# Three edits to a written order: a pair's tail rows stored by GpSimd instead of ScalarE, another pair's stored earlier on the SP queue, and one narrowing step ahead of a copy

## The chip, the core and the metric

The kernel runs on one core of a Trainium2 chip. The core's engines (TensorE for matrix products, VectorE, ScalarE, GpSimd, and SyncE, whose queue issues most of the DMAs) each take their own instructions in order and wait for one another through semaphores. The metric is the device time of one execution in microseconds (us). Where several executions are timed, the median is given. A profile is one execution with a record of every instruction; its times start at the first instruction of the span. In its rows PE is TensorE's matrix product, PEld its weight load, DVE VectorE, ACT ScalarE, POOL GpSimd, SP SyncE, and a q behind the name (SPq, ACTq) is the engine's sequencer, which issues DMAs.

## The reference

Attention without a softmax, with a normalisation per head, followed by a gated linear unit with a causal convolution of five taps. There are 8 sequences (batch) of 576 tokens, 8 heads of 64, so 512 channels.

```
kv  = einsum('bhsd,bhse->bhde', k, v)
out = einsum('bhsd,bhde->bhse', q, kv)
x   = out / sqrt(mean(out*out, -1) + 1e-6) * g_norm     # heads side by side: (8, 576, 512)
gate_pre = sum over k of conv_w[k] * x shifted by 4 - k tokens
y   = (sigmoid(gate_pre) * (x @ w_val)) @ w_out
```

q, k, v and g_norm are float32; the three weights come as float64, which the kernel narrows itself.

## The kernel before

The whole kernel is a list of steps, PLAN (lines 19 to 226), written out by hand in one order. A loop at line 882 calls one small function for each step, so the list's order is the order in which each engine gets its instructions, and nothing is rescheduled. A step such as `store 0 8` is the function with its arguments; numbers behind an @ pick the buffers that the step's new tiles take.

Work goes by sequence b (0 to 7) and, from the output product on, by pairs i (0 to 3) of two sequences. For one sequence: load_half and load_q bring k, v and q; kv_product and kv_copy make kv; turn_q transposes q on VectorE; raw_pair and raw_tail make out in chunks c of 128 tokens (chunk 4 is the tail of 64); square (ScalarE), sums (VectorE) and powers (GpSimd) give the norms and normalise scales; turn_blocks (VectorE) and move_blocks b a (line 663: four DMAs, two issued by GpSimd and two by SP) put the transposed x of tokens 128 a to 128 a + 127 into xT, while the tail goes through TensorE (turn_x, keep_x, then halo). Then gate_start, gate_tap and gate_end make the gate. x_sums, val_fast and val_keep make x @ w_val with seven products of half size where a plain split takes eight; val_fast 3 1 0, the first of sequence 3, reads tokens 0 to 287 of xT. gated multiplies the two.

For a pair of sequences the output product works likewise: token_sums, fast_product i p n (line 818, seven products n for each of four p) and fast_keep i p n (line 841), which copies or adds a bank into one of the ot buffers. Of these there are four, numbered 0 to 3, of 128 x 512. The tails of both sequences of a pair, 64 tokens each, go together as c = 8: out_product i 8 (L784), keep_out i 8 (L792), which copies them into an ot buffer, and a store.

A store is four DMAs of 32 rows (64 KB each). It is issued by SP unless a queue is given. The step that next writes the same ot buffer must wait until all four have landed:

- first pair: keep_out 0 8 takes ot buffer 0, and fast_keep 0 2 1 (L851, ScalarE) takes it next. In PLAN store 0 8 stands on line 106, behind load_half k 5 1 and move_blocks 3 2, which issue on SP too.
- last pair: keep_out 3 8 takes ot buffer 1, and fast_keep 3 3 1 (L851) takes it next. store_side 3 8 on line 222 issues its four DMAs on ScalarE's queue, ahead of fast_keep 3 3 0 (L849) on the same engine. That copy takes ot buffer 2, which store 3 1 reads before, and the products behind it need the bank that it copies out. store_last (line 862) splits the last two stores between SP and ScalarE.

The weights are narrowed at the start by steps narrow_weight key tile n: n = 0 and n = 4 to 7 on VectorE, n = 1 to 3 on ScalarE. keep_cw (line 452) is three small VectorE operations that copy the transposed convolution weights and the column gcol out of a bank; gcol is read by n = 7 of wval (L425).

Of the kernel before, what the change touches and what calls it, by code (L numbers as in the profile page):

```python
# [27 lines left out]
narrow_weight cw 0 5 @ 0; narrow_weight cw 0 6 @ 1; raw_half 0 2 0 @ 4; narrow_weight cw 0 7;  # L28
narrow_weight wval 0 1; raw_half 0 3 1; narrow_weight wval 0 5 @ 2; raw_half 0 0 1; narrow_weight wval 0 6 @ 3;
square 0 3 @ 0; raw_half 0 4 1 @ 6; square 0 0 @ 1; turn_cw @ 1; sums 0 3 @ 0 0; raw_half 0 2 1;  # L30
narrow_weight wval 0 2; keep_cw; raw_half 0 4 0; powers 0 3; narrow_weight wval 1 0 @ 0; load_half v 1 0;
square 0 2 @ 2; raw_half 0 1 0 @ 5; sums 0 0; square 0 4 @ 0; narrow_weight wval 0 3;
narrow_weight wval 1 5 @ 0; raw_half 0 1 1; sums 0 4; start_warm 1 256 @ 0; narrow_weight wval 1 1;
load_half k 1 0; sums 0 2; square 0 1 @ 1; narrow_weight wval 0 4; powers 0 2; narrow_weight wval 1 2;
# [65 lines left out]
gate_start 2 3 @ 2; turn_blocks 3 1; token_sums 0 1 0 @ 0; square 3 4 @ 2; out_product 0 8 @ 3;  # L100
load_half k 5 0 @ 0; gate_start 2 1 @ 1; turn_q 4 1; kv_copy 4 0; kv_copy 4 1; sums 3 4; token_sums 0 1 1;
turn_q 4 3; val_keep 2 1 5; turn_blocks 3 3; raw_pair 4 1 @ 7 6; keep_out 0 8 @ 0; token_sums 0 1 3 @ 2;
move_blocks 3 1; val_keep 2 0 5; raw_pair 4 3 @ 4 2; gate_tap 2 1 3; square 4 0 @ 0; store 0 2; powers 3 4;
fast_product 0 2 0 @ 3; sums 4 0 @ 0 0; square 4 2 @ 1; gate_tap 2 3 3; gate_start 2 0 @ 3; powers 4 0;
fast_product 0 3 0 @ 0; load_half k 5 1 @ 0; gate_tap 2 1 2; fast_keep 0 2 0 @ 2; move_blocks 3 2;
normalise 3 4 @ 1; fast_product 0 2 2; token_sums 0 1 2; square 4 1 @ 2; gate_tap 2 2 3; store 0 8;
fast_product 0 3 1 @ 1; fast_keep 0 3 0 @ 1; fast_keep 0 2 2; gate_tap 2 0 3; square 4 3 @ 0;
fast_product 0 3 2; normalise 4 0 @ 0; sums 4 1; move_blocks 3 0; fast_product 0 3 3; gate_tap 2 2 2;
powers 4 1; fast_product 0 2 1 @ 5; sums 4 2; fast_keep 0 3 2; fast_keep 0 3 1 @ 3; gate_tap 2 0 2;
# [120 lines left out]
def kernel(  # L230
# [11 lines left out]
    nc = tc.nc  # L242
# [62 lines left out]
    wval = const.tile([P, NK, C], FP32, name="wval")  # L305
# [559 lines left out]
    def store(i, c, queue=nc.sync, blocks=range(HB)):  # L865
        ot = st["ot", i, c]
        for j in blocks:
            bb, n = divmod(c * HB + j, NJ * HB) if c < 2 * NJ else (j // 2, NJ * HB + j % 2)
            queue.dma_start(out=rows_out[2 * i + bb, n], in_=ot[j * TB:(j + 1) * TB, :])  # L869

    def store_side(i, c):
        store(i, c, nc.scalar)

    steps = {f.__name__: f for f in (
        load_half, load_q, load_q_rows, stage_weight, narrow_weight, turn_cw, keep_cw, start_warm, warm_up,
# [1 line left out]
        turn_x, keep_x, turn_blocks, move_blocks, halo, gate_start, gate_tap, gate_end, val_product, keep_val, gated,  # L877
        val_sums, x_sums, val_fast, val_keep, out_product, keep_out, weight_sums, token_sums, fast_product, fast_keep,
        store, store_side, store_last)}
    with tc.manual_schedule():  # L880
        set_up()
# [35 lines left out]
```

## Time and profile before

| what | us |
|---|---|
| median of three runs | 301.51 (301.21 to 302.94) |
| the profiled execution | 302.35 |
| its span, first to last instruction | 300.6 |
| DMA: share of 16 engines' time, hardware queue of SP | 56.7% |
| DMA: the same, GpSimd's software queue | 4.6% |
| DMA: the same, ScalarE's hardware queue | 2.2% |

The profiled execution is 0.84 us longer than the median of the runs, and 1.75 us of it lie around the span. A share of busy time is a mean over stages with different limits, so what an edit is worth is read at its place. The chain of waits follows the work that ended last back from the end: each piece is what released the one behind it, so time outside the chain is not time that the end waits for.

### The profile page before, as it was taken

What the parts mean: (1) busy time and instruction counts of PE and PEld (TensorE: products, weight loads), DVE (VectorE), ACT (ScalarE), POOL (GpSimd) and SP (SyncE); (2) the same over time, 40 slices, a digit from 0 to 9 for tenths busy, and PEclk for the clock granted to TensorE, in tenths of its full rate; (3) what the DMA queues carried; (4) which work ended last, traced back from release to release, by engine and by line L of the source; (5) the groups of instructions that cost most, each with busy time, mean ns of one, the idle gap of its engine ahead of it and who ended that gap; (6) DMA issues with size and microseconds to landing.
All of it is one profiled execution on the core that took longest, in us unless ns stands there. A gap on an engine that the chain in (4) does not pass through costs nothing.

```text
span 300.6 us, 8644 instructions
## 1 busy us (share of the span) xinstructions
PE 288.7 (96%) x3279; PEld 225.6 (75%) x3279; DVE 270.4 (90%) x483; ACT 198.5 (66%) x621; POOL 116.9 (39%) x127
## 2 busy tenths in 40 slices
PE   7988999999999998999999999999999999999993
PEld 4766788878887766788887767788877588788572
DVE  1699999999999998989999999998999999999712
ACT  2899999999685865883587476656567654614230
POOL 3056064862666059310692486040593081000000
PEclk9999999999999999999999999999999999999999
DMA  7999984886599558985969479653651162230344
GB/s 269 379 388 410 257 253 141 247 266 203 131 249 289 155 137 225 240 229 123 276 166 306 97 197 328 167 142 106 142 129 37 26 152 68 55 88 0 87 118 111
DMA packets 32073, 55.51 MB, mean 185 GB/s; under 512 B 6166, under 2 KB 14358, under 8 KB 32032
## 3 DMA queue, kind: packets, MB, share of 16 engines
q1 hardware_dynamic: 29328, 49.50, 56.7%
q0 software_dynamic: 1632, 3.17, 4.6%
q10 hardware_dynamic: 1072, 2.29, 2.2%
q8 instruction: 26, 0.43, 0.7%
q14 instruction: 15, 0.12, 0.1%
HBM read 39.21 MB, written 9.44 MB: 162 GB/s over the span
## 4 chain that ended last, share of the span: by engine, by line
PE 57%; DVE 16%; DMA 8%; ACT 6%; SPq 6%; issue 3%; POOL 2%; ACTq 1%; DVEq 0%
PE bank L746 22%; PE bank L837 18%; PE bank L697 6%; DVE gate L685 5%; DMA qs<-in_q_dram 5%; PE bank L475 4%; SPq L869 4%; DMA out_dram<-ot 3%; PE bank L550 3%; PE bank L784 2%; SPq L357 2%; POOL rt L616 2%; DVE ss L606 2%; ACT qT L533 1%; ACT x L635 1%
## 5 line engine op out<-in xcount | busy, mean ns | idle before, releaser
L685 DVE SCALAR_TENSOR_TENSOR gate<-xT,cwT,gate 128x576 f32<-128x576 f32 x128 | 100.1, 808 | 0.3
L616 POOL TENSOR_TENSOR rt<-ss,mhalf 128x8 f32<-128x8 f32 (+3 forms) x38 | 70.7, 1878 | 56.3 <-DVE ss L606 56.1
L635 ACT ACTIVATE x<-bank,rt 128x64 f32<-128x64 f32 x252 | 57.0, 414 | 2.3 <-POOL rt L616 2.3
L668 POOL DMA_DIRECT2D xT<-y x48 | 26.7, 561 | 73.0 <-issue 28.4
L837 PE MATMUL bank<-wsum,w 128*128 128x256 f32 x192 | 46.8, 381 | 0.6 <-ACT ot L849 0.6
L837 PEld LDWEIGHTS bank<-wsum,w 128*128 128x128 f32 x192 | 36.0, 190 | 7.2 <-ACT ot L849 1.1
L746 PE MATMUL bank<-xs,vsum 128*128 128x288 f32 x144 | 38.0, 409 | 0.1
L746 PEld LDWEIGHTS bank<-xs,vsum 128*128 128x128 f32 x144 | 26.9, 190 | 8.1 <-ACT gv L755 0.5
L697 PE MATMUL bank<-xT,wval 128*128 128x288 f32 x128 | 32.8, 409 | 0.0
L837 PE MATMUL bank<-wout,gv 128*128 128x256 f32 x128 | 32.7, 383 | 0.0
L692 ACT ACTIVATE gate<-gate 128x576 f32<-128x576 f32 x32 | 22.7, 719 | 12.8 <-DVE gate L685 12.8
L599 ACT ACTIVATE sq<-bank 128x256 f32<-128x256 f32 (+1 forms) x70 | 22.4, 401 | 9.5 <-PE bank L550 9.4
L697 PEld LDWEIGHTS bank<-xT,wval 128*128 128x128 f32 x128 | 23.7, 190 | 6.3 <-DVE wval L425 0.2
L847 DVE TENSOR_TENSOR ot<-bank,ot 128x256 f32<-128x256 f32 (+1 forms) x32 | 17.2, 548 | 12.3 <-PE bank L837 6.2
L679 ACT ACTIVATE gate<-xT,cwT 128x576 f32<-128x576 f32 x32 | 25.6, 823 | 2.4 <-DMA xT<-y 1.1
L837 PEld LDWEIGHTS bank<-wout,gv 128*128 128x128 f32 x128 | 23.8, 190 | 3.6
L606 DVE TENSOR_REDUCE ss<-sq 128x8 f32<-128x520 f32 (+1 forms) x40 | 24.9, 630 | 1.4 <-ACT sq L599 1.0
L746 PE MATMUL bank<-xT,wval 128*128 128x288 f32 x96 | 25.7, 408 | 0.1
L710 DVE TENSOR_TENSOR gv<-gv,gate 128x576 f32<-128x576 f32 x32 | 23.3, 750 | 0.6 <-ACT gate L692 0.6
L746 PEld LDWEIGHTS bank<-xT,wval 128*128 128x128 f32 x96 | 17.9, 190 | 4.9 <-issue 0.5
L550 PEld LDWEIGHTS bank<-kv,qT 64*64 64x64 f32 x1008 | 16.5, 135 | 5.4 <-issue 2.8
L475 PEld LDWEIGHTS bank<-v,k 64*64 64x64 f32 x1008 | 16.1, 135 | 3.7 <-issue 2.5
(90 smaller groups left out, 460.8 us busy)
## 6 DMA issues: line engine op xcount, KB each, us to landing
qs<-in_q_dram SPq DMA_DIRECT2D x96, 140.0 KB, 4.1
out_dram<-ot SPq DMA_DIRECT2D x136, 64.0 KB, 1.8
k<-in_k_dram SPq DMA_DIRECT2D x14, 576.0 KB, 5.8
v<-in_v_dram SPq DMA_DIRECT2D x12, 576.0 KB, 5.7
xT<-y SPq DMA_DIRECT2D x48, 64.0 KB, 2.5
xT<-y POOLq DMA_DIRECT2D x48, 64.0 KB, 2.7
y<-in_moe_w_val_dram SPq DMA_DIRECT2D x4, 512.0 KB, 11.9
w<-in_moe_w_out_dram SPq DMA_DIRECT2D x4, 512.0 KB, 10.2
```

The lines of the kernel that those rows point to most:

```text
L475: nc.tensor.matmul(st["kvps", b][s][r * D:(r + 1) * D, i], st["k", b, i][rows, r, cols], st["v", b, i][rows, r, cols], start=(j == 0), sto ...
L550: nc.tensor.matmul(st["raw", b, c][r][cols, to * D:(to + 1) * D], st["qT", b][rows, hp, first:first + D], kvs[b % 2][rows, hp, :], start=T ...
L606: nc.vector.reduce_sum(out=st["ss", b][:, FIRST[c]:FIRST[c] + n], in_=st["sq", b, c][:, 0:n], axis=AX.X)
L616: nc.gpsimd.tensor_tensor(out=st["rt", b][:, which], in0=st["ss", b][:, which], in1=mhalf[:, which], op=ALU.pow)
L635: nc.scalar.activation(out=x[:, to * D:(to + 1) * D], in_=raw[:, h * D:(h + 1) * D], func=AF.Copy, scale=root[:, to:to + 1])
L668: (nc.sync if i % 2 else nc.gpsimd).dma_start(out=xTs[b % 2][i * TB:(i + 1) * TB, :, first:first + P], in_=y[a * TB:(a + 1) * TB, i])
L679: nc.scalar.activation(out=gate[:], in_=xTs[b % 2][:, jt, HALO:SX], func=AF.Copy, scale=cwT[:, K - 1, jt:jt + 1])
L685: nc.vector.scalar_tensor_tensor(out=gate[:], in0=xTs[b % 2][:, jt, tap * TB:tap * TB + S], scalar=cwT[:, tap, jt:jt + 1], in1=gate[:], op ...
L697: nc.tensor.matmul(val[:], wval[:, kc, jt * P:(jt + 1) * P], xTs[b % 2][:, kc, HALO + n * SV:HALO + (n + 1) * SV], start=(kc == 0), stop=( ...
L710: nc.vector.tensor_tensor(out=both, in0=both, in1=st["gate", b, jt][:], op=ALU.mult)
L746: nc.tensor.matmul(st[bank, "val", b, mj][:], weights_[:, k], tokens()[:, k], start=(n in (0, 1, 3) and k == 0), stop=(k == NK // 2 - 1), ...
L837: nc.tensor.matmul(st[bank, i, p], tokens()[:, k], weights_[:, k], start=(n < 2 and k == 0), stop=(k == NK // 2 - 1), skip_group_check=True)
```

## The change

Two steps of the list move and one function changes; the same operations are done, in the same buffers.

- store 0 8 moves up, from behind gate_tap 2 2 3 to directly behind store 0 2. On SP it passes load_half k 5 1 and the two SP moves of move_blocks 3 2.
- keep_cw moves down, past raw_half 0 4 0, powers 0 3 and narrow_weight wval 1 0. On VectorE it passes one instruction, the n = 0 step of that weight (L399).
- store_side, used once for the last pair's tails, issues on GpSimd's queue instead of ScalarE's.

```
-narrow_weight wval 0 2; keep_cw; raw_half 0 4 0; powers 0 3; narrow_weight wval 1 0 @ 0; load_half v 1 0;
+narrow_weight wval 0 2; raw_half 0 4 0; powers 0 3; narrow_weight wval 1 0 @ 0; keep_cw; load_half v 1 0;
...
-move_blocks 3 1; val_keep 2 0 5; raw_pair 4 3 @ 4 2; gate_tap 2 1 3; square 4 0 @ 0; store 0 2; powers 3 4;
-fast_product 0 2 0 @ 3; sums 4 0 @ 0 0; square 4 2 @ 1; gate_tap 2 3 3; gate_start 2 0 @ 3; powers 4 0;
-fast_product 0 3 0 @ 0; load_half k 5 1 @ 0; gate_tap 2 1 2; fast_keep 0 2 0 @ 2; move_blocks 3 2;
-normalise 3 4 @ 1; fast_product 0 2 2; token_sums 0 1 2; square 4 1 @ 2; gate_tap 2 2 3; store 0 8;
+move_blocks 3 1; val_keep 2 0 5; raw_pair 4 3 @ 4 2; gate_tap 2 1 3; square 4 0 @ 0; store 0 2; store 0 8;
+powers 3 4; fast_product 0 2 0 @ 3; sums 4 0 @ 0 0; square 4 2 @ 1; gate_tap 2 3 3; gate_start 2 0 @ 3;
+powers 4 0; fast_product 0 3 0 @ 0; load_half k 5 1 @ 0; gate_tap 2 1 2; fast_keep 0 2 0 @ 2; move_blocks 3 2;
+normalise 3 4 @ 1; fast_product 0 2 2; token_sums 0 1 2; square 4 1 @ 2; gate_tap 2 2 3;
...
     def store_side(i, c):
-        store(i, c, nc.scalar)
+        store(i, c, nc.gpsimd)
```

TensorE's order is unchanged. VectorE's changes by the one instruction, ScalarE's list is shorter by the four DMAs and GpSimd's longer by them, behind its last other work; SP's changes only around the moved store.

## The prediction

> **What bounds the kernel now.** I read the busy shares first, then stretches of the span, then the chain of waits in the two places where the diff moves a store, then the queues around them.
>
> ```profile
> span 300.6 us, 8644 instructions
> PE 288.7 (96%) x3279; PEld 225.6 (75%) x3279; DVE 270.4 (90%) x483; ACT 198.5 (66%) x621; POOL 116.9 (39%) x127
> ...
> 110.00:130.00 20.00, 18.66 (x167) 15.26 (x164) 18.11 (x29) 14.19 (x57) 12.96 (x16) 1.00 0.86 220
> 130.00:190.00 60.00, 59.94 (x664) 46.31 (x663) 59.13 (x103) 38.19 (x128) 29.82 (x33) 1.00 0.76 211
> ...
> 270.00:300.60 30.60, 25.41 (x114) 18.99 (x112) 15.72 (x27) 8.06 (x20) 0.00 (x0) 0.99 0.30 78
> ```
>
> The first two lines are of the page, the other three a view by stretch (length, then busy time of PE, PEld, DVE, ACT, POOL, the granted clock, the DMA share, GB/s). TensorE is busy 96% of the span and in the middle (130 to 190 us) all but 0.06 us of 60, with VectorE all but 0.87. So there is little to gain except where TensorE stands still: 1.34 us between 110 and 130 us, and the last stretch. Both are places of this change.
>
> **The first pair's tails (store 0 8).** These rows are the chain, then timelines of TensorE, VectorE and SP.
>
> ```profile
> 116.33 3.35 DMA out_dram<-ot
> ...
> 119.82 0.38 ACT ot L851
> ...
> 115.29 2.75 PE L837 MATMUL bank<-wsum,w 128*128 128x256 f32 x12
> ...
> 120.25 1.13 PE L837 MATMUL bank<-wout,w 128*128 128x256 f32 x4 [1.34 <-ACT ot L851]
> ...
> 122.43 2.18 PE L746 MATMUL bank<-xT,wval 128*128 128x288 f32 x8
> ...
> 127.24 1.28 PE L475 MATMUL bank<-v,k 64*64 64x64 f32 x72
> ...
> 120.22 0.42 DVE L847 TENSOR_TENSOR ot<-bank,ot 128x256 f32<-128x256 f32 x1 [0.85 <-ACT ot L851]
> ...
> 129.31 0.42 DVE L606 TENSOR_REDUCE ss<-sq 128x4 f32<-128x260 f32 x1 [1.03 <-ACT sq L599]
> ...
> 112.86 0.52 SPq L347 DMA_DIRECT2D k<-in_k_dram  x1
> 113.43 1.24 SPq L668 DMA_DIRECT2D xT<-y  x2
> 114.77 2.15 SPq L869 DMA_DIRECT2D out_dram<-ot  x4
> 116.96 2.92 SPq L668 DMA_DIRECT2D xT<-y  x4
> ```
>
> The copy at L851 (fast_keep 0 2 1) writes the ot buffer that keep_out 0 8 filled, so it waits until store 0 8 has landed, at 116.33 + 3.35 = 119.68. TensorE's next product waits for that copy: 1.34 us idle, VectorE 0.85. The product that the copy reads is the first third of the group at 115.29, 2.75 / 3 = 0.92 us long, so the copy could start near 116.2.
>
> ```profile
> L869 SPq DMA_DIRECT2D out_dram<-ot x4: 425/500/591, 114.8 to 116.3; - x4
> ...
> DMA to landing us min/median/max: 3.3/3.8/4.3
> ...
> L869 SPq DMA_DIRECT2D out_dram<-ot x4: 420/545/1612, 109.5 to 112.3; - x4
> ...
> DMA to landing us min/median/max: 1.9/2.7/3.6
> ...
> k<-in_k_dram SPq DMA_DIRECT2D x14, 576.0 KB, 5.8
> ...
> xT<-y SPq DMA_DIRECT2D x48, 64.0 KB, 2.5
> ```
>
> The edit puts the four issues in the slot at 112.86. At 0.50 us each (their median) the last starts at 112.86 + 3 x 0.50 = 114.36. Landing then takes between the 1.9 us of the store just ahead and the 4.3 us that these very DMAs took behind the load of k; I take 2.7, the median of the store just ahead, since the two would be neighbours: landed at 117.1. At 4.3 it is 118.7. TensorE is due 1.34 us before 120.25, at 118.9, and the copy lies 0.43 us ahead of it (119.82 to 120.25), so it must start by 118.5. At 2.7 the whole 1.34 us go; at 4.3 the copy starts at 118.8 (0.14 us after landing, as now) and TensorE at 119.2, so 1.0 us go.
>
> What is moved past: the load of k (one issue, 0.52) and SP's two moves of move_blocks 3 2 now issue up to 2.15 us later, the length of the four issues in their old place. SP runs from 112.86 to 119.88 without a gap, so its four moves at 116.96 keep their place. The load starts at about 115 and lands 5.8 later, at 120.8; kv_product 5 1 wants it at 127.24 - 1.34 = 125.9, so 5 us cover that. The moves issue from about 115.6 to 116.2 and land 2.5 later, by 118.7; the first product that reads them is that at 122.43, which then comes at 121.1, so 2.4 us cover them. Of the later four, the first two (move_blocks 3 0) feed the same product: the second issues at about 116.96 + 2.92 / 4 = 117.7 and lands at 120.2, a cover of only 0.9 us; the other two carry tokens 384 to 511, which that product doesn't read. GpSimd's half of move_blocks 3 2 is on its own queue and isn't moved past.
>
> Who is late next? VectorE gains 0.85 here, and at 129.31 it waits 1.03 us for a square that TensorE's product releases. With both 1.34 earlier, it arrives 0.85 earlier and waits 0.54, so the whole 1.34 us is kept there. After that neither has slack to lose against the other, and SP itself waits for VectorE:
>
> ```profile
> SPq L668 <- DVE y L660: 5.8, 2, 4.7
> ```
>
> A 4.7 us wait of the DMA queue between 118 and 175 us means that the queue isn't what sets the pace there, and moves along. I take **1.3 us**, between 1.0 and 1.34.
>
> **The last pair's tails (store_side 3 8).** The chain near the end, the landing of the last DMA ahead of it, TensorE, ScalarE, and GpSimd's DMAs of the whole run:
>
> ```profile
> 287.62 0.37 ACTq L869
> ...
> 290.98 0.38 ACT ot L849
> ...
> 291.41 4.60 PE bank L837 x20
> ...
> L869 SPq DMA_DIRECT2D out_dram<-ot x1: 435/435/435, 287.1 to 287.1; - x1
> ...
> DMA to landing us min/median/max: 3.5/3.5/3.5
> ...
> 291.41 1.13 PE L837 MATMUL bank<-wsum,w 128*128 128x256 f32 x4 [0.58 <-ACT ot L849]
> ...
> 294.10 1.03 PE L837 MATMUL bank<-wout,w 128*128 128x256 f32 x4
> ...
> 293.44 0.37 ACT L851 COPY ot<-bank 128x256 f32<-128x256 f32 x1 [0.49 <-PE bank L837]
> ...
> L668 POOL DMA_DIRECT2D xT<-y x48: 551/551/638, 77.5 to 246.9; - x48
> ...
> DMA to landing us min/median/max: 2.0/2.7/5.5
> ```
>
> ScalarE spends 287.62 to about 290.9 issuing the four stores, and the copy L849 (fast_keep 3 3 0) stands behind them. That looks like 3.3 us, but is not. First, TensorE has other work: it idles only 0.58 us before 291.41, the ceiling. Second, the same copy writes the ot buffer of store 3 1, whose last DMA was issued at 287.1 and took 3.5 us to land, 290.6. So with ScalarE free it starts near 290.7 instead of 290.98: **0.3 us**, the floor, unless that landing too comes down towards the usual 1.8 us of a store, in which case 0.58. Part of its 3.5 us may be the four ScalarE stores beside it; part is not known from these rows. I take 0.35, and from there it reaches the end: the chain goes on with 20 products in one piece, and the last stores follow them.
>
> The added side: four GpSimd issues at 0.55 us from 287.7, the last at 289.35, landing 2.7 later at 292.1. GpSimd has no work at all after 270 us (the third stretch above), so nothing queues behind them but the kernel's end, and the end is over 7 us away. Who waits is fast_keep 3 3 1 (L851 at 293.44, then 293.1), which writes the same ot buffer: 1 us of cover.
>
> Here a rule speaks against the edit. The Trainium skill, "SBUF — State Buffer", section "SBUF: two separate sides", says that GpSimd cannot write the descriptors of its DMAs while VectorE runs an operation in a two-port mode, such as a float32 copy from SBUF to SBUF, and advises the ScalarE or SP queue.
>
> ```profile
> 287.46 0.42 DVE L847 TENSOR_TENSOR ot<-bank,ot 128x256 f32<-128x256 f32 x1 [3.68 <-DMA out_dram<-ot]
> 290.00 0.69 DVE L847 TENSOR_TENSOR ot<-bank,ot 128x512 f32<-128x512 f32 x1 [2.11 <-PE bank L837]
> ```
>
> If by that rule both of these held GpSimd for their whole length, the last landing would come 1.11 us later, 293.2, and cost 0.1 of the 0.35; they are additions with one operand from a bank, and no row here shows the rule at work.
>
> **keep_cw and the narrowing step.** On VectorE the three small operations of keep_cw, from 17.05 on, and the narrowing step behind them change places:
>
> ```profile
> 17.05 0.16 DVE L454 TENSOR_SCALAR gcol<-bank 128x1 f32<-128x1 f32 x1
> ...
> 17.59 0.43 DVE L399 TENSOR_SCALAR wexp<-y 128x512 uint32<-128x512 uint32 x1
> ...
> 21.61 0.73 DVE L425 SCALAR_TENSOR_TENSOR wval<-ot,gcol,wexp 128x512 f32<-128x512 f32 x1
> ```
>
> The block keeps its length, gcol is late by 0.43 us and is first read at 21.61, nearly 4 us on. The narrowing step comes 0.54 earlier (17.59 to 17.05), but stage after stage of its weight waits for ScalarE in an order that isn't changed. Zero; for a bound I take one such small operation, 0.16, either way.
>
> **Sum.** 1.3 + 0.35 + 0 = 1.65 us. The profiled execution took 302.35 us, its span 300.6 and 1.75 around it; less 1.65 is 300.7. The median of the runs is 301.51, 0.84 below the profiled one; less 1.65 it is **299.9**.
>
> **Rivals.**
>
> 1. The gain near 119 us is given back, by moves of x that land late or by a load of q or v that TensorE and VectorE now reach 1.3 us sooner. For: the DMA share there is 0.86, and the landing times above reach 4.3. Against: the covers of 0.9 to 5 us, and SP's own waits. Only the end's 0.35 is left: 301.2.
>
> 2. Slower than before: GpSimd's stores land late and hold up fast_keep 3 3 1. The place is L851 at 293.44, the product at 294.10 behind it. The first GpSimd DMAs of the run, after idleness like this, have this row:
>
> ```profile
> cw<-in_g_norm_dram POOLq DMA_DIRECT2D x2, 0.2 KB, 5.9
> ```
>
> At 5.9 the last lands at 295.25, L851 starts at 295.4, its product at 295.4 + 0.43 = 295.8, which is 1.7 after 294.10; with 1.3 gained before, 0.4 slower: 301.9. It ends slower than before once the landing passes 5.5 us, and with the first gain lost as well it is 303.2. Against: the median is 2.7, and DMA is 0.30 busy at the end.
>
> 3. The edit at the end removes nothing, since the landing of store 3 1 stays the last to come and GpSimd's packets delay it as ScalarE's did: 301.51 - 1.3 = 300.2, inside the forecast.
>
> **How the numbers follow.** The forecast, with rival 3 in it, gets 0.68 (299.5 to 300.4 with the terms' bounds and a few tenths of scatter), rival 1 0.17, rival 2 0.09, and 0.06 goes to what no row shows, half each way. The range 299.1 to 302.0 takes the forecast, rival 1 and most of rival 2. A measurement of this kernel can tell a difference of about 1%, 3 us: no gain worked out here is so large (1.34 + 0.58 = 1.92 at most), and only rival 2 with the first gain lost comes near it on the other side. So within 1% 0.90, faster 0.04, slower 0.06.
>
> **What would show it.** In the changed profile: SP's four stores directly behind those of store 0 2, landing by 118.5; no wait of TensorE for L851 near 119; VectorE's wait before L606 near 128 about 0.5; the stretch from there to 270 shifted by 1.3 as a whole; L849 no longer behind stores, but still behind the landing of store 3 1, TensorE's wait before it 0.2 to 0.3; GpSimd's four issues near 286.4 to 288.6, landing ahead of L851. It is wrong if a new wait of TensorE or VectorE over 0.3 us appears between 119 and 180, or if L851 names a DMA near the end.

## The result and the profile after

| | before | after |
|---|---|---|
| median of 21 runs each, us | 301.61 (299.82 to 304.72) | 300.22 (298.35 to 303.43) |
| ratio after / before, 95% interval | | 0.9952 (0.9932 to 0.9972) |
| the profiled execution, us | 302.35 | 299.51 |
| its span, us | 300.6 | 297.7 |

The change gains about 0.5%, 1.45 us (0.0048 x 301.61). That is inside the 1% called no change in the prediction, but the interval doesn't reach 1.

The page of after begins so:

```profile
span 297.7 us, 8649 instructions
PE 287.1 (96%) x3279; PEld 225.1 (76%) x3279; DVE 270.5 (91%) x483; ACT 198.6 (67%) x621; POOL 120.3 (40%) x131
```

The view by stretch of after (length, busy time of PE, PEld, DVE, ACT, POOL, granted clock, DMA share, GB/s):

```profile
110.00:130.00 20.00, 19.03 (x171) 15.82 (x167) 18.59 (x30) 14.93 (x59) 15.47 (x16) 1.00 0.88 231
130.00:190.00 60.00, 59.94 (x672) 46.27 (x674) 59.52 (x104) 38.49 (x129) 28.80 (x33) 1.00 0.73 206
270.00:297.70 27.70, 23.37 (x105) 17.31 (x103) 14.26 (x24) 6.84 (x16) 2.02 (x4) 1.00 0.33 86
```

TensorE still idles 0.97 us between 110 and 130 us (20 - 19.03), where 1.34 were to go whole. TensorE's timeline of after shows that this is another wait:

```profile
119.62 1.03 PE L837 MATMUL bank<-wout,gv 128*128 128x256 f32 x4
...
121.83 2.18 PE L746 MATMUL bank<-xT,wval 128*128 128x288 f32 x8 [0.97 <-DMA xT<-y]
```

The first group, the product behind the copy L851, waited 1.34 us before; it has no wait in brackets now. The group of val_fast 3 1 0 behind it waits 0.97 us for a move of x. VectorE's timeline says the same:

```profile
119.32 0.42 DVE L847 TENSOR_TENSOR ot<-bank,ot 128x256 f32<-128x256 f32 x1
...
128.71 0.42 DVE L606 TENSOR_REDUCE ss<-sq 128x4 f32<-128x260 f32 x1 [1.41 <-ACT sq L599]
```

Its 0.85 us at L847 are gone, and its wait for the square is 1.41 where it was 1.03. Time taken out at one wait has gone into the next; TensorE's 0.97 us is a new wait of over 0.3 us between 119 and 180 us, which the prediction named as a sign of being wrong. SP's timeline, and the moves' issues with their landing:

```profile
109.53 5.30 SPq L869 DMA_DIRECT2D out_dram<-ot  x8
114.93 0.40 SPq L347 DMA_DIRECT2D k<-in_k_dram  x1
115.37 3.86 SPq L668 DMA_DIRECT2D xT<-y  x6
119.28 0.60 SPq L347 DMA_DIRECT2D v<-in_v_dram  x1
```

```profile
L668 SPq DMA_DIRECT2D xT<-y x6: 585/598/607, 115.4 to 118.6; - x6
...
DMA to landing us min/median/max: 3.2/4.2/4.8
```

(The three numbers are minimum, median and maximum, of the issue in ns and of the landing in us.) The eight stores stand together, the load of k next, and all six moves directly behind it. They land 4.2 us after issue, not 2.5.

At the end the profiled execution shows most of what could be had. Rows of TensorE, of ScalarE, of the last DMA of store 3 1 and of GpSimd's stores, each from its own view of after:

```profile
288.99 1.13 PE L837 MATMUL bank<-wsum,w 128*128 128x256 f32 x4 [0.21 <-ACT ot L849]
```

```profile
288.57 0.37 ACT L849 COPY ot<-bank 128x256 f32<-128x256 f32 x1 [3.02 <-DMA out_dram<-ot]
```

```profile
L869 SPq DMA_DIRECT2D out_dram<-ot x1: 432/432/432, 285.0 to 285.0; - x1
...
DMA to landing us min/median/max: 3.4/3.4/3.4
```

```profile
L869 POOL DMA_DIRECT2D out_dram<-ot x4: 498/504/532, 285.8 to 287.4; - x4
...
DMA to landing us min/median/max: 1.9/2.3/2.8
```

The copy L849 no longer stands behind issues; it stands behind the landing of store 3 1, which again takes 3.4 us (285.04 + 3.43 = 288.47 in the chain). TensorE waits 0.21 for it, 0.58 before. GpSimd's stores have all landed by 287.4 + 2.8 = 290.2 at the latest, ahead of the copy L851.

Where the 2.9 us of span between the two profiles went is read from the start of the same TensorE product in both. Up to 118 us they agree; the first product of val_fast 3 1 0 comes 0.60 sooner (122.43 before, 121.83 after), a product at 220 us 2.08 sooner, that behind L849 2.42 sooner (291.41, 288.99), the end 2.9. So half of it, 1.5 us, arises between 122 and 220 us, where the diff changes nothing; TensorE's idle time in 130 to 222 us (92 less busy) is 0.91 before and 0.06 after. The experiments say how far that is the change's.

### The profile page after: what moved, and what is told of

Same layout as the page of the kernel before. It is cut to its first block, busy times and chain, and to the rows that moved or that the text cites. A ratio compares the mean times of both kernels' runs of the same rounds, so it can differ in the third digit from the quotient of the medians.

```text
span 297.7 us, 8649 instructions
## 1 busy us (share of the span) xinstructions
PE 287.1 (96%) x3279; PEld 225.1 (76%) x3279; DVE 270.5 (91%) x483; ACT 198.6 (67%) x621; POOL 120.3 (40%) x131
## 3 DMA queue, kind: packets, MB, share of 16 engines
q0 software_dynamic: 1760, 3.43, 5.1%
## 4 chain that ended last, share of the span: by engine, by line
PE 79%; DMA 7%; DVE 5%; SPq 3%; POOL 2%; ACT 2%; issue 1%; ACTq 0%; DVEq 0%
PE bank L837 28%; PE bank L746 28%; PE bank L697 6%; PE bank L475 5%; PE bank L784 5%; PE bank L550 4%; DMA v<-in_v_dram 4%; POOL rt L616 2%; DMA out_dram<-ot 1%; PE bank L562 1%; DMA xT<-y 1%; PE bank L647 1%; DMA qs<-in_q_dram 1%; DVE ss L606 1%; SPq L668 1%; DVE gate L685 1%
## 5 line engine op out<-in xcount | busy, mean ns | idle before, releaser
L847 DVE TENSOR_TENSOR ot<-bank,ot 128x256 f32<-128x256 f32 (+1 forms) x32 | 17.2, 548 | 10.5 <-PE bank L837 9.5
L550 PE MATMUL bank<-kv,qT 64*64 64x64 f32 x1008 | 18.4, 221 | 0.3 <-ACT x L635 0.2
```

What stands on the lines that cost most here:

```text
L550: nc.tensor.matmul(st["raw", b, c][r][cols, to * D:(to + 1) * D], st["qT", b][rows, hp, first:first + D], kvs[b % 2][rows, hp, :], start=T ...
```

## The experiments

The theory: the store's new place removes the wait at L851, but the load of k now starts just ahead of the moves of x that TensorE needs next, and they land behind it. Rivals: the moves are late whatever the place of k; or the wait removed was not the store's but only the execution's. At the end: GpSimd takes ScalarE's issues out of the copy's way, and the landing of store 3 1 is what remains; the rival is that the edit there does nothing.

Idle times are TensorE's: in 110 to 130 us (20 less busy), in 130 to 222 us (92 less busy), and the wait before the product behind L849. They are of one profiled execution each. Medians and ratios are of the timed runs, and a ratio is taken against runs of the kernel before on the same chip. The kernels were not all timed on one chip, so kernels are compared by their ratios and not by their medians.

| kernel | median us (runs) | ratio, 95% interval | 110-130 | 130-222 | behind L849 |
|---|---|---|---|---|---|
| before | 301.61 (21) | | 1.34 | 0.91 | 0.58 |
| before, once more | 302.64 (1) | | 1.89 | 0.72 | 0.65 |
| before + keep_cw moved | 302.09 (12) | 1.0006 (0.9983 to 1.0029) | 1.63 | 0.63 | 0.48 |
| before + GpSimd's stores | 301.12 (12) | 0.9988 (0.997 to 1.0006) | 1.05 | 0.85 | 0.43 |
| before + store 0 8 moved | 300.32 (12) | 0.9963 (0.9939 to 0.9987) | 0.04 | 0.89 | 0.35 |
| after | 300.22 (21) | 0.9952 (0.9932 to 0.9972) | 0.97 | 0.06 | 0.21 |
| after, once more | 299.77 (1) | | 0.81 | 0.55 | none |
| after, k behind the moves | 299.75 (12) | 0.9942 (0.9913 to 0.9972) | 2.09 | 0.47 | 0.41 |
| after, k early | 299.11 (9) | 0.9933 (0.991 to 0.9955) | 0 | 0.31 | 0.20 |
| before, k early | 299.41 (5) | 0.9923 (0.9895 to 0.9951) | 0 | 0.36 | 0.43 |
| after, store 3 1 earlier | 299.04 (1) | | 0.37 | 0.45 | none |
| after, last tails on SP | 301.00 (10) | 0.998 (0.9958 to 1.0002) | 0.46 | 0.02 | 0.22 |
| after, k early, store 3 1 earlier | 298.41 (6) | 0.9892 (0.9863 to 0.9921) | 0 | 0.01 | none |
| the same, last tails on ScalarE | 299.28 (10) | 0.9929 (0.9904 to 0.9954) | 0 | 1.21 | 0.39 |

Six ratios lie outside the range that was expected of them: keep_cw moved by 0.0001, k behind the moves by 0.0002, the last one by 0.0004, last tails on SP (slower than expected), and before with k early and after with both further moves (faster). Each measured interval still reaches into the expected range.

### Each edit by itself

Only store 0 8 moved, in the kernel before:

```
-... square 4 0 @ 0; store 0 2; powers 3 4;
+... square 4 0 @ 0; store 0 2; store 0 8; powers 3 4;
...
-... square 4 1 @ 2; gate_tap 2 2 3; store 0 8;
+... square 4 1 @ 2; gate_tap 2 2 3;
```

> Only store 0 8 is moved up. Theory (most of the gain comes from here, but not the 1.3 us at once): TensorE's 1.34 us wait for L851 near 119 is gone and a wait of about 1 us for the moves of x takes its place near 121, so that only 0.4 to 0.6 us are gained there and the rest further on; about 1.0 us faster than the kernel before, ratio 0.996 to 0.998. Rival (the move of the store is worth nothing and the gain comes from elsewhere): ratio 0.999 to 1.001, and the offset against the kernel before stays under 0.2 us from 130 us on.

Only GpSimd's queue for the last tails (`store(i, c, nc.gpsimd)` in store_side):

> Only the last pair's tails go to GpSimd's queue. Theory: TensorE's wait for L849 at the end falls from 0.58 to 0.2 us, since the landing of store 3 1 stays as the last to come; 0.35 us faster, ratio about 0.9988. Rival (the end is worth over 1 us): ratio under 0.997. Other rival (GpSimd's stores land late): L851 at the end waits for a DMA and the ratio is over 1.

Only keep_cw behind narrow_weight wval 1 0:

> Only keep_cw and the narrowing step change places. Theory: nothing, ratio 0.9995 to 1.0005 as far as the scatter lets it be seen, and the rows of VectorE from 18 us on at their old times within 0.2 us. Rival (it is a hidden part of the gain): 0.3 us or more faster, seen as an offset of that size from 25 us on.

The store alone brings 0.9963, the largest part; keep_cw alone 1.0006, with its interval on both sides of 1. GpSimd alone, 0.9988, can't be told from no change by its time. The three multiplied give 0.9957, after has 0.9952, so the edits neither help nor hinder one another by much. For GpSimd there is TensorE's timeline of that kernel:

```profile
290.51 1.13 PE L837 MATMUL bank<-wsum,w 128*128 128x256 f32 x4 [0.43 <-ACT ot L849]
```

0.43 is less than the 0.58 before (0.2 was expected), but not by more than two executions of one kernel differ. With the store alone moved, the stretch and the moves' landing were:

```profile
110.00:130.00 20.00, 19.96 (x171) 16.48 (x171) 19.54 (x32) 15.68 (x60) 13.91 (x16) 1.00 0.86 228
```

```profile
L668 SPq DMA_DIRECT2D xT<-y x6: 585/599/601, 115.0 to 118.2; - x6
...
DMA to landing us min/median/max: 2.6/3.6/4.4
```

Here TensorE waits for nothing, though the order on SP is that of after. So the wait for the moves isn't there in every execution, and its size had to be found from several.

### Both kernels once more

> The kernel before once more, for a second profile. Theory (its waits for L851 near 119 and for L849 at the end belong to the kernel, while those of VectorE near 179 and 203 change with the execution): 1.0 to 1.7 us and 0.4 to 0.6 us at the first two again, the others anywhere from 0 to 1 us. Rival (all of them belong to the kernel): all within 0.1 us of the first profile.

> The changed kernel once more. Theory: no wait for L851 near 119 again; the wait for xT near 121, 0.97 us in the first profile and 0 in the run with the store moved alone, comes out anywhere between 0 and 1 us; the wait at the end is 0.2 to 0.35 us again. Rival (the wait for xT belongs to the changed kernel): 0.9 to 1 us again.

The stretch of the kernel before, profiled again, then that of after:

```profile
110.00:130.00 20.00, 18.11 (x184) 14.82 (x177) 17.67 (x28) 13.57 (x57) 14.47 (x16) 1.00 0.81 211
```

```profile
110.00:130.00 20.00, 19.19 (x174) 15.94 (x167) 18.74 (x30) 15.05 (x59) 15.59 (x16) 1.00 0.88 226
```

The waits come back at the same places with other sizes: 1.89 us at the store before, 0.81 at the moves after. Between 130 and 222 us before idles 0.72 and after 0.55, so most of the difference between 0.91 and 0.06 in the first pair did not come back in the second.

### The load of k behind the moves

```
-... load_half k 5 1 @ 0; gate_tap 2 1 2; fast_keep 0 2 0 @ 2; move_blocks 3 2;
+... gate_tap 2 1 2; fast_keep 0 2 0 @ 2; move_blocks 3 2;
...
-fast_product 0 3 2; normalise 4 0 @ 0; sums 4 1; move_blocks 3 0; fast_product 0 3 3; ...
+fast_product 0 3 2; normalise 4 0 @ 0; sums 4 1; move_blocks 3 0; load_half k 5 1 @ 0; fast_product 0 3 3; ...
```

> The changed kernel with one more step moved: load_half k 5 1 goes behind move_blocks 3 0, so that on SP four moves of x that stood behind 576 KB of k stand ahead of it. Theory (the new wait near 121 us comes from the order on SP's queue, since the moves land behind the load): TensorE's 0.97 us wait for xT is gone or under 0.3, and the kernel is 0.5 to 1 us faster than the changed one, ratio to the kernel before about 0.992 to 0.994. Rival (the 16 DMA engines are simply full there and the order does not matter): a wait of 0.8 to 1 us stays, ratio about 0.995. Other rival (the load of k then comes late): TensorE waits for k at kv_product 5 1 near 126 us.

The moves ahead of the load are quick and the wait for xT is gone, but TensorE's timeline of this execution (302.92 us, one of the two slowest of the twelve) has a new wait:

```profile
127.46 1.75 PE L475 MATMUL bank<-v,k 64*64 64x64 f32 x72 [2.09 <-DMA qs<-in_q_dram]
```

The releaser named is inferred; the load of v, which this product reads, was issued at 119.29 and landed at 127.33, 8.0 us later and 0.13 ahead of the product (with only the store moved it took 4.6). Why it took so long in this execution isn't shown. The load of k, which the other rival would have had late, landed at 121.86, well ahead. The median, 299.75, isn't told apart from that of after.

### The load of k early

The other half of k issues at 104 us. Each half has a buffer of its own, and the last product that reads this half's buffer before, kv_product 4 1, is done at about 104.4 us, so the load can issue directly behind that of the other half:

```
-load_half k 5 0 @ 0; gate_start 2 1 @ 1; ...
+load_half k 5 0 @ 0; load_half k 5 1 @ 0; gate_start 2 1 @ 1; ...
...
-powers 4 0; fast_product 0 3 0 @ 0; load_half k 5 1 @ 0; gate_tap 2 1 2; ...
+powers 4 0; fast_product 0 3 0 @ 0; gate_tap 2 1 2; ...
```

> The changed kernel with load_half k 5 1 directly behind load_half k 5 0, so on SP ahead of the first moves of x for sequence 3, where SP stood idle from 104.8 to 108.2 us. Theory (the load of 576 KB is what the moves stand behind): the four moves that landed at 120.8 to 121.8 us land before 120, no wait of TensorE near 121, none at kv_product 5 1 near 126 either, and 0.3 to 0.9 us faster than the changed kernel, ratio to the kernel before 0.992 to 0.9945. Rival (the DMA engines are full around 120 us in any case): the moves land where they did and the ratio stays at 0.995 to 0.9965.

The stretch, the moves and VectorE's wait for the square, from three views of that kernel:

```profile
110.00:130.00 20.00, 20.00 (x171) 16.73 (x172) 19.82 (x32) 15.80 (x60) 14.11 (x16) 1.00 0.81 205
```

```profile
L668 SPq DMA_DIRECT2D xT<-y x6: 585/600/608, 114.8 to 118.0; - x6
...
DMA to landing us min/median/max: 2.0/2.2/2.5
```

```profile
127.42 0.42 DVE L606 TENSOR_REDUCE ss<-sq 128x4 f32<-128x260 f32 x1 [0.18 <-ACT sq L599]
```

The six moves issue within 0.6 us of where they did in after, and land in 2.2 us instead of 4.2. On SP nothing else about them differs, so it was the 576 KB ahead of them. TensorE has no idle time left in the stretch. The load itself now issues at about 104.8, 10 us sooner.

The load delays more than its own queue. GpSimd issues moves too, on another queue, and in the kernel with k behind the moves it issued one at 117.36 us, the time at which SP issued the load of k there. It landed behind the load, which took 4.5 us, and not after 2.1 like the one that GpSimd had issued 0.6 us sooner:

```profile
L668 POOL DMA_DIRECT2D xT<-y x2: 551/568/586, 116.8 to 117.4; - x2
...
DMA to landing us min/median/max: 2.1/3.4/4.7
```

So it is the load in flight that counts, and not only the order on SP's queue.

Then the same one line in the kernel before, with the store in its old place:

> The kernel before, its store 0 8 in its old place, with load_half k 5 1 alone moved directly behind load_half k 5 0. Theory (store 0 8 landed late because 576 KB of k stood ahead of it on the same queue, and the moves of x did so after the change): its DMAs take about 2 us to land instead of 3.3 to 4.3, L851 starts before 118.6, TensorE waits under 0.3 us near 119 and not at all near 121; 1.2 to 2 us faster than the kernel before, ratio 0.993 to 0.996, without moving the store. Rival (it is the place of the store in SP's order that counts): the store is issued from 114.2 on and L851 still holds TensorE up by over 0.8 us.

SP's timeline and the store's landing:

```profile
112.88 1.27 SPq L668 DMA_DIRECT2D xT<-y  x2
114.25 1.93 SPq L869 DMA_DIRECT2D out_dram<-ot  x4
```

```profile
L869 SPq DMA_DIRECT2D out_dram<-ot x4: 419/422/532, 114.2 to 115.8; - x4
...
DMA to landing us min/median/max: 2.0/2.2/2.6
```

The store issues within 0.6 us of its place in the kernel before (114.8 to 116.3 there) and lands in 2.2 us instead of 3.8. ScalarE's copy L851 still waits 1.4 us for that landing, but TensorE waits for nothing. Its place was not the fault: the load of k ahead of it was. Moving the store out from behind the load cured the symptom, and since the load then issues 2.1 us later (112.86 before, 114.93 after), it stands right ahead of the moves instead.

### The end: order and queue

Store 3 1, whose last DMA takes 3.4 us to land, goes ahead of stores 3 2 and 3 0:

```
-out_product 3 8 @ 3; fast_keep 3 0 6; fast_keep 3 1 5; fast_keep 3 0 5; store 3 2; ...
+out_product 3 8 @ 3; fast_keep 3 0 6; store 3 1; fast_keep 3 1 5; fast_keep 3 0 5; store 3 2; ...
...
-store 3 1; fast_product 3 2 4; ...
+fast_product 3 2 4; ...
```

> The changed kernel with store 3 1 on SP directly behind store 3 3, ahead of stores 3 2 and 3 0. Theory (what is left of the wait at the end is the landing of store 3 1, the last of twelve DMAs in a row, caught behind a 16 KB transfer on the queue that the page calls instruction): L849 no longer waits for a DMA and TensorE's wait of 0.21 us before the product behind it is gone, 0.2 us. Rival (L849 waits for something else): the wait stays. The store that is now last, 3 0, may take 3.4 us to land in turn, and then the copy L792 waits for it.

ScalarE's waits of that kernel (in all, times, longest):

```profile
ACT ot L792 <- DMA out_dram<-ot: 1.4, 1, 1.4
...
ACT ot L851 <- DMA out_dram<-ot: 0.6, 1, 0.6
```

TensorE no longer waits behind L849. (This kernel was run once, so it has no ratio.) The waits of ScalarE that are left, for store 3 0 and for GpSimd's store, cost TensorE nothing.

Who issues the last tails: SP in the place of GpSimd.

> The changed kernel with the last pair's tails on SP's queue instead of GpSimd's. Theory (all that counts at the end is that ScalarE is free for L849; who issues the stores does not matter while they land ahead of L851): TensorE's wait before the product behind L849 stays at 0.1 to 0.45 us, SP has room for four issues between store 3 1 and store 3 4, ratio to the kernel before as with GpSimd, 0.994 to 0.9965. Rival (GpSimd's queue is itself the gain, SP would be in the way): stores 3 4 and 3 5 start 1 us or more later than on GpSimd's side and the kernel is 0.3 us or more slower than the changed one.

The wait behind L849 is 0.22, as with GpSimd, but the ratio is 0.998. Its interval overlaps that of after (0.9958 to 1.0002 and 0.9932 to 0.9972), so by time alone the loss isn't shown. In the profiled execution it can be followed. SP's waits of this kernel after 283 us have one that after doesn't:

```profile
SPq L869 <- DMA out_dram<-ot: 1.5, 1, 1.5
```

TensorE ends at 293.64 us here and at 293.58 in after, but the last DMA of the run is issued at 296.25, in after at 294.88. In the built program the DMAs of SP and ScalarE take turns on eight semaphores, and each issue waits until the DMA before it on its semaphore has landed. Four more DMAs in that round put one of SP's last stores on the semaphore of a ScalarE store that landed at 295.41; SP's issue follows at 295.43. In both kernels of the table with store 3 1 earlier and GpSimd's stores, SP has a wait of the same kind, of 0.6 us. What was expected to change nothing met a wait that neither theory had.

Then the two gains together, k early and store 3 1 earlier, on after:

> The changed kernel with both further moves: load_half k 5 1 behind load_half k 5 0, and store 3 1 directly behind store 3 3. Theory (the two gains lie in different places and add): TensorE waits neither near 119 and 121 nor before the product behind L849, ratio to the kernel before 0.9920 to 0.9935. Rival (store 3 1 ahead moves the wait to L792, L851 or the last stores): a wait of over 0.2 us in the last 12 us, ratio 0.993 to 0.995.

Its stretches:

```profile
110.00:130.00 20.00, 20.00 (x179) 16.69 (x172) 19.82 (x32) 15.80 (x60) 14.22 (x16) 1.00 0.82 210
130.00:222.00 92.00, 91.99 (x1120) 73.92 (x1119) 91.03 (x159) 58.51 (x197) 42.93 (x46) 1.00 0.68 187
```

At 0.9892 it beats both kernels; the upper end, 0.9921, lies below the lower end of after. The step from 0.9952, some 1.8 us, is more than the waits of 0.5 and 0.25 us that were taken away; where the rest comes from stays open. And with ScalarE issuing the last tails, as before the change:

> The fastest version so far (load_half k 5 1 behind load_half k 5 0, store 3 1 behind store 3 3), but with the last pair's tails on ScalarE's queue as in the kernel before. Theory (at the end two things hold L849, the landing of store 3 1 and ScalarE's own issuing, and each hides the other's removal): with the landing out of the way, L849 still stands behind four issues on ScalarE, TensorE waits 0.4 to 0.8 us for it, and the kernel is 0.3 to 0.7 us slower than with GpSimd, ratio to the kernel before 0.9900 to 0.9925. Rival (the landing alone counted, and GpSimd is worth nothing): no wait of TensorE there, ratio 0.988 to 0.990.

ScalarE's timeline there:

```profile
287.88 1.80 ACTq L869 DMA_DIRECT2D out_dram<-ot  x4
289.72 0.37 ACT L849 COPY ot<-bank 128x256 f32<-128x256 f32 x1 [1.87 <-issue]
```

With store 3 1 out of the way, the copy waits for ScalarE's own issues, 1.87 us, and TensorE 0.39 where it waited for nothing. The two ratios, 0.9929 and 0.9892, are some 1.1 us apart, more than 0.39, but their intervals overlap (0.9904 to 0.9954 and 0.9863 to 0.9921), so the trace shows the wait and the time doesn't show what it costs. Where the rest is stays open: the profiled execution, 301.02, is the slowest of the ten, so its 1.21 us of idle time between 130 and 222 doesn't stand for the median.

## Why the prediction was right, and where it was not

**Time.** 299.9 was forecast, 300.22 measured, inside the range, and within 1% as was held likeliest. The sum, 1.65 us, compares with 1.45. But the first term was larger on paper than on the chip, and a part that the sum didn't have helped to make up for it: the two terms as measured below, 0.95 and 0.25, make 1.2 of the 1.45. That the total came out so near is in part luck.

**Store 0 8.** The store's own step held, as its row of after shows:

```profile
L869 SPq DMA_DIRECT2D out_dram<-ot x4: 420/423/757, 112.7 to 114.4; - x4
...
DMA to landing us min/median/max: 2.2/2.5/2.5
```

The last issue is at 114.4 (114.36 in the sum) and has landed by 116.9 (117.1), and TensorE's and VectorE's waits at 119 us are gone. What failed is the step on what is moved past: "The moves issue from about 115.6 to 116.2 and land 2.5 later", and with them move_blocks 3 0 landing at 120.2, "a cover of only 0.9 us". The 2.5 was the median of all SP moves of the run; none of the five of those moves whose landing is on record came that soon (3.2 us at the least). The kernel before had the price already: its two SP moves directly behind the same load took 4.6 and 4.9 us. The prediction allowed the store up to 4.3 us behind that load, but not the moves.

```profile
L668 SPq DMA_DIRECT2D xT<-y x2: 592/600/607, 113.4 to 114.1; - x2
...
DMA to landing us min/median/max: 4.6/4.8/4.9
```

The records of each DMA in five kernels with this order on SP, and one with k early, show what sets the landing (us):

| kernel | load of k: issued, landed | second SP move of move_blocks 3 0: issued, landed | product of val_fast 3 1 0 starts |
|---|---|---|---|
| after | 114.93, 120.41 | 117.30, 121.49 | 121.83 |
| after, once more | 114.86, 120.50 | 117.22, 121.38 | 121.73 |
| last tails on SP | 115.01, 120.19 | 117.47, 121.50 | 121.85 |
| store 3 1 earlier | 114.70, 119.35 | 117.07, 120.66 | 121.01 |
| before + store 0 8 moved | 114.52, 119.14 | 116.88, 120.28 | 120.63 |
| after, k early | early | 116.69, 119.16 | 120.61 |

In all of the first five the load lands first and the move 0.9 to 1.3 us behind it, and the product starts 0.34 to 0.35 us after the move. The load takes between 4.6 and 5.6 us, and so the product comes on time or a whole microsecond late. With k early the move lands in 2.5 us and the product starts when TensorE is free. This is the first rival's mechanism: it took the gain back in part, 0.04 to 0.97 us, not whole as that rival had it.

The Trainium skill, "DMA: Bandwidth & Descriptors", section "Two DMAs through the same engine are not ordered", states that the descriptors in one queue of one DMA engine start in order, and that when a later one completes an earlier one need not have finished writing. So the order of starting fits these traces, but the order of landing is only what these traces show: no SP move behind the load has a landing on record ahead of the load's. The same page of the Trainium skill, section "Issuing engines are not separate DMA queues", says that DMAs issued by different engines run on the same 16 DMA engines and interleave. The trace agrees: GpSimd's two moves of block 3 3, issued at 116.9 and 117.5 us, landed in a median of 4.0 us in after and 2.2 with k early.

The size, then: with the store late TensorE idles 1.34, 1.89, 1.63 and 1.05 us in the stretch, 1.48 in the mean; with the store moved and k still ahead of the moves 0.97, 0.81, 0.46, 0.37 and 0.04, 0.53 in the mean. The term is 0.95 us where 1.3 was taken. VectorE's wait for the square, due to fall to 0.54, is 0.46 with the store alone moved and 0.18 with k early, where the moves were in time, and 1.41 in after, where they were not.

**The stretch from 128 to 270 us.** Shifted by 1.3 as a whole was forecast. In the first pair of profiles it isn't: the same products come 0.6 to 0.7 us sooner from 122 to 179 us, and 2.08 at 220. TensorE's idle time in 130 to 222 us is 0.91, 0.72, 0.63 and 0.85 with the store late, 0.78 in the mean, and 0.06, 0.55, 0.02, 0.45 and 0.89 with it moved, 0.39 in the mean. That is some 0.4 us gained that no step of the sum had; but the values within either group lie so far apart that it stays open whether the change makes it or the choice of executions.

**The last pair's tails.** Right, with the floor nearer than the ceiling: TensorE's wait was 0.58, 0.65, 0.48, 0.35 and 0.43 with ScalarE issuing, and 0.21, none, 0.43, 0.41, 0.20 and 0.22 with GpSimd or SP, so about 0.5 becomes 0.25, where 0.35 was taken off. The step behind it is seen more sharply in the start of L849 behind the last landing of store 3 1. That is 0.38 to 0.39 us in four executions with ScalarE issuing (0.11 in the one of keep_cw moved), and 0.10 in all five on record with GpSimd or SP: 0.28 us, the floor. The landing of store 3 1 stays the last to come. It takes 3.4 us with GpSimd's stores beside it as it took 3.5 with ScalarE's, and neither is what delayed it (see the last section), so the third rival has the landing right, but not its cause, nor that the edit removes nothing. By the time alone the gain isn't shown (0.997 to 1.0006).

**GpSimd's stores.** The second rival needed a landing later than 5.5 us: it was 2.3 in the median, 2.8 at most, and the issues took 0.50 us each against the 0.55 taken. Of the rule of the Trainium skill, "SBUF — State Buffer", section "SBUF: two separate sides", the profile of after shows nothing either way: GpSimd issues from 285.84 to 287.86, and VectorE does nothing between its additions at 285.42 (0.42 us) and 287.96. In the two kernels with store 3 1 earlier and GpSimd's stores, an addition of 0.69 us with an operand from a bank (at 287.79 and 286.99) does lie within GpSimd's four issues, and they take 2.02 and 2.01 us there as they take 2.02 in after. So additions of this kind did not hold GpSimd up; the prediction had counted with that as the worst case.

**keep_cw.** Zero, as far as its time can tell (1.0006, 0.9983 to 1.0029) and by the start of VectorE's timeline of after, where the narrowing step comes first and gcol, behind a step of 0.42 us, is still 3.6 us ahead of its reader:

```profile
16.82 0.42 DVE L399 TENSOR_SCALAR wexp<-y 128x512 uint32<-128x512 uint32 x1
...
17.73 0.15 DVE L456 TENSOR_SCALAR gcol<-gcol 128x1 f32<-128x1 f32 x1
...
21.48 0.74 DVE L425 SCALAR_TENSOR_TENSOR wval<-ot,gcol,wexp 128x512 f32<-128x512 f32 x1
```

## What to carry to other kernels

When a small transfer comes late, look at what large transfer is issued just ahead of it, on its own queue or another, before moving it: here one 576 KB load delayed whichever 64 KB transfers followed it by 1.6 to 2 us. Moving that load by four lines of the list took the wait away whole (0.9923), where moving the store passed part of it on (0.9963); the traces show this, while the intervals of the two ratios overlap. For a transfer that an edit puts behind a load, take as its landing time the load's own landing plus its place behind it, not the median of its kind over the run. And before trusting a difference between two profiles in a stretch that an edit doesn't touch, profile both kernels again.

## What the runs showed of the hardware that was not expected

The landing of one and the same DMA differs much between executions: the load of k issued at about 115 us took 4.6, 4.6, 5.2, 5.5 and 5.6 us in the five kernels above, that of v 4.6 and 8.0. That spread of a microsecond is as large as the cover of 0.9 us that the prediction relied on.

The last DMA of store 3 1 takes 3.4 to 3.5 us in these two profiles, where the stores ahead of it take 1.7. In the packet records a 16 KB transfer, of the queue that the page calls instruction (26 of them in the run, 0.43 MB), lies at that time: at 288.16 us for 1.38 us before, at 286.05 for 1.36 after. In before, 30 of the 32 data packets of that DMA have started by 288.4 us, and the last two start at 289.53 and 289.75, when the 16 KB transfer has just ended (289.55); in after the first of the last two starts at 287.39, at the end of that transfer at 287.41. In all ten executions in which store 3 1 is in its old place and the landing is on record, it comes 1.05 to 1.08 us behind the end of that transfer, whether ScalarE, GpSimd or SP issues the tails. With store 3 1 earlier no store there takes 3.4 us, all of SP's stores issued from 281 to 284.3 land in 1.7. So the instruction transfer is what holds the DMA up, as far as the order of the packets shows it; no run took the transfer away.

That DMAs of two engines wait for one another through the semaphores that the program shares out among them (1.5 us of waiting with the last tails on SP) belongs to the program and not to the chip, but it shows on no list of steps: it is found only in the waits.
